# First tile of a fused attention and expert kernel: decoded weights grouped in pairs, and where their transfers are issued

## The chip, the cores and the metric

The kernel runs on one core of a Trainium2 chip. The metric is the device time of one execution in microseconds (us), as the median of several runs. The core has five engines that run their own instruction streams and wait for each other through semaphores: TensorE (PE, the matmuls), VectorE (DVE), ScalarE (ACT), GpSimd (POOL) and SyncE (SP, which here only starts DMAs). ACT can start DMAs too. Memory transfers are carried by 16 DMA engines that all queues share.

## The reference, cut to what matters

```
# attention without softmax: 8 batches, 8 heads, 576 tokens, head size 64
kv  = einsum('bhsd,bhse->bhde', k, v)
out = einsum('bhsd,bhde->bhse', q, kv)
x   = out / sqrt(mean(out*out) + 1e-6) * g_norm        # -> 4608 tokens x 512
# first expert layer: w_in 512 x 2048, w_out 2048 x 512
h = x @ w_in
P = a0 + a1*h + a2*h*h + a3*h*h*h
Q = 1 + |b0|*|h| + |b1|*h*h
x = (P / (Q + 1e-6)) @ w_out
# second expert layer: w_gate, w_val 512 x 1536, w_out 1536 x 512
g = x @ w_gate
return (g * sigmoid(g) * (x @ w_val)) @ w_out
```

All of it is float32.

## The kernel before, in words

**Tiles and steps.** The first expert layer goes over nine tiles of 512 tokens. One tile has 16 steps, one for each block of 128 hidden columns; a step s counts through all tiles. In step s, PE multiplies x with block f of w_in (`h_mm`), ACT and DVE compute P/Q from the sum in PSUM (`g_step`, `g_finish`), and two steps later (LAG = 2) PE multiplies the activated block `ghl` with block f of w_out (`y_mm`). Between them, `attn_*` prepares x of the next tile.

**Exact products.** A float32 operand is held as a high and a low part that PE takes in its fast float32 form; a product is three matmuls (high·high, low·high, high·low; lines 110 to 118). The low part is the operand less its high part: ACT copies the high part, and DVE or POOL subtracts.

**Weights.** They arrive as 64-bit numbers, 0.5 MB for a block of 512 values in each of 128 partitions, and are decoded on the chip in the first tile alone: an ACT pass (`w_exp`), a DVE shift (`w_shift`, TENSOR_SCALAR `wraw<-wraw`), a DVE join (`wa_joins`, SCALAR_TENSOR_TENSOR `wraw<-wraw`), then the high part on ACT (`wt<-wraw`) and the subtraction on DVE (`wt<-wraw,wt`), both in `w_hi`. Later tiles only read the decoded `wt`. `wa_sets` is the list of what is decoded together, one entry a step. Before, blocks i0 and i1 of w_in come in the head of the program, and entry s then holds block i(s+2) of w_in and block o(s) of w_out: one 1024 column shift, join and ACT pass, and for each block its own 512 column copy and subtraction.

**Blocks left whole.** The w_out blocks named in `WHOLE` (11, 12, 13) are not split in the first tile: one DVE join writes them as plain float32 (`wf`), their `ghl` is not split either, and the product is one matmul in float32 (line 501) in place of three fast ones. `w_halve` splits them in steps 4, 7 and 10 of the second tile, and `w_move` moves one by a DMA in step 12.

**Transfers.** `wa_fetch` starts the transfers of an entry. All are started from SP's queue, between the loads of `kvm`/`kvr` (k and v, for the kv products that run beside the first tile) and of `q` for the next tile. A tile name has buffers, and a load waits until its buffer was read for the last time.

**Order.** Nothing is scheduled by a tool: each engine runs its instructions in the order in which the code issues them (line 1143). In the loop over steps that is: `h_mm(s)`, `y_mm(s-2)`, the kv products, `g_step` (the activation of step s, with the joins, the `ghl` of step s-1, the copies and subtractions in between), and at the end of the step `wa_scale` (the ACT pass and the shift of the next entry) and `wa_fetch`.

Of the kernel before, what the change touches and what calls it, by code (L numbers as in the profile page):

```python
# [8 lines left out]
F32 = mybir.dt.float32  # L9
# [6 lines left out]
P = 128  # L16
# [25 lines left out]
def fused_kernel(ctx: ExitStack, tc: tile.TileContext, kv_main, kv_left, q_t, w_in, w_out, w_gate, w_val, w_o2, ab, g_norm, out):  # L42
# [38 lines left out]
    rows = w_p.tile([1, 3, P], F32, tag="w3", name="rows")  # L81
# [7 lines left out]
    for n in (18, 20, 22, 24, 26, 28, 3):  # L89
        w_p.tile([P, 2, N], F32, tag=f"w{n}", name="place")  # L90
    kvf = w_p.tile([P, HP, P], F32, tag="w31", name="kvf")

    def act(out, in_, func=AF.Copy, **kw):
        nc.scalar.activation(out=out, in_=in_, func=func, **kw)  # L94
# [25 lines left out]

    W = {}
    raws = []
    WHOLE = (11, 12, 13)

    def w_views(st):
        wi = st.bitcast(I32).rearrange("p (n two) -> p n two", two=2)
# [27 lines left out]
    ring_w = {}

    def w_tile(n):
        kind, f, _ = wa_src[n]
        if kind == "o" or f >= 2 * (RING - 4):
            return w_p.tile([P, 2, N], F32R, tag=f"w{n}", name="wt")
        if f % 2 == 0:  # L160
            ring_w[f // 2] = ring_p.tile([P, 2, 2, N], F32R, tag=f"r{f // 2}", name="wt")
        return ring_w[f // 2][:, f % 2]

    def w_hi(st, n, key, eng=nc.vector):
        wt = W[key] = w_tile(n)
        act(wt[:, 0, :], w_views(st)[2])
        return partial(sub, eng, wt[:, 1, :], w_views(st)[2], wt[:, 0, :])


    wa_src = [("i", f, w_in[f]) for f in range(LAG)]  # L170
    wa_sets = [(f,) for f in range(LAG)]
    for f in range(NF1):
        n = len(wa_src)
        wa_src += [("i", f + LAG, w_in[f + LAG])] if f + LAG < NF1 else []
        wa_src.append(("o", f, w_out[f]))
        wa_sets.append(tuple(range(n, len(wa_src))))
    wa_raw = ((at_p, "hl"), (s_p, "stg"), (at_p, "r0"), (w_p, "w5"), (w_p, "w7"), (x_p, "x11"))
    wa_home = [3, 4, *(5, 0, 1) * 4, 0, 1, 2, 1]
    wa_n = [0]

    def wa_fetch():
        if wa_n[0] < len(wa_sets):
            ns, (pool, tag) = wa_sets[wa_n[0]], wa_raw[wa_home[wa_n[0]]]
            r = pool.tile([P, 2 if tag in ("hl", "stg", "x11") else 1, N], I64, tag=tag, name="wraw")
            for j, n in enumerate(ns):
                nc.sync.dma_start(out=r[:, j, :], in_=wa_src[n][2])
            raws.append((ns, r[:, :len(ns), :].rearrange("p a n -> p (a n)")))
            wa_n[0] += 1

    def wa_hi(eng=nc.vector):  # L190

        ns, r = raws.pop(0)
        js = [(j, n) for j, n in enumerate(ns) if not whole(n)]
        return [partial(w_hi, r[:, j * N:j * N + N], n, wa_src[n][:2], eng) for j, n in js]

    def wa_scale(*parts):
        for _, r in raws[:1]:
            for part in parts or (w_exp, w_shift):
                part(r)

    def whole(n):
        kind, f, _ = wa_src[n]
        return kind == "o" and f in WHOLE

    def wa_joins():
        ops = []
        for ns, r in raws[:1]:
            if not any(whole(n) for n in ns):
                return join_ops([r])
            for j, n in enumerate(ns):  # L210
                lo, hi, _ = w_views(r[:, j * N:j * N + N])
                out = hi
                if whole(n):
                    wf = W[wa_src[n][:2]] = w_p.tile([P, N], F32, tag=f"w{n}", name="wf")
                    out = wf.bitcast(I32)
                ops.append(partial(stt, out, hi, 3, lo, ALU.logical_shift_left, ALU.bitwise_or))
        return ops

    def w_halve(f):
        wf, k = W["o", f], WHOLE.index(f)  # L220
        pool, tag = (w_p, f"w{2 * WHOLE[k - 1] + 3}") if k else (at_p, "r0")
        wt = W["o", f] = pool.tile([P, 2, N], F32R, tag=tag, name="wt")
        act(wt[:, 0, :], wf)
        return [partial(sub, nc.vector, wt[:, 1, :], wf, wt[:, 0, :])]

    def w_move():
        wf = W["o", WHOLE[0]]
        wt = W["o", WHOLE[0]] = w_p.tile([P, 2, N], F32R, tag=f"w{2 * WHOLE[-1] + 3}", name="wt")
        nc.sync.dma_start(out=wt.bitcast(F32), in_=wf.bitcast(F32))
# [19 lines left out]
    kv_lefts = [w_p.tile([P, HP, 2, P], F32, tag=f"w{n}", name="kvr") for n in (26, 27, 19)]

    def kv_tag(n):
        slots = (24, 25, 28, 29, 30, 20, 21, 22, 23)
        return f"w{slots[n] if n < 5 else slots[(n - 5) % 9] if n < 28 else (23, 24, 25, 28)[n - 28]}"

    def kv_load(k):

        for n in range(kv_n[0], min(kv_n[0] + k, len(kv_jobs))):
            b, hp = kv_jobs[n]
            tag = kv_tag(n)
            if kv_last.get(tag, -1) >= kv_n[1] or hp == 0 and kv_n[1] < 4 * b - 8:  # L260
                return
            kv_last[tag] = n
            m = w_p.tile([P, 4, 2, P], F32, tag=tag, name="kvm")
# [46 lines left out]
            nc.sync.dma_start(out=kvp[diag(j), 1 - j::2, :], in_=kvf[diag(1 - j), j::2, diag(1 - j)])  # L310

    def q_load(hp):
        q = q_in[0, hp] = w_p.tile([P, N], F32, tag=f"w{20 + hp}", name="q")
        nc.sync.dma_start(out=q, in_=q_t[0, hp])

    def q_load4(T, g):
# [136 lines left out]
    def attn_tail(c):  # L453
        T, f = at(c)
        if T is None:
            return
        if T == 1:
            if f == 2:
                kv_place()
            if f in (1, 4):  # L460
                q_load4(1, f // 3)
            elif f == 10:
                r_spread(1)
            elif f == 12:
# [62 lines left out]
    def g_finish(s, ops, his=()):  # L527
        if s not in mid:
            return []
        e1, e2, e3 = mid.pop(s)  # L530
        stt(e1, e1, 1.0 + EPS_Q, e2, ALU.add, ALU.mult)
        stt(e3, e3, na[:, 0:1], e2, ALU.add, ALU.mult)
        run(ops, len(ops))
        w = s in WHOLE
        hl = g_p.tile([P, N] if w else [P, 2, N], F32 if w else F32R, tag="g", name="ghl")
        stt(hl if w else e3, e1, 2.0, e3, ALU.subtract, ALU.mult)
        lows = [hi() for hi in his[:1]]
        if not w:
            split(hl, e3, nc.gpsimd)
        hl_t[s] = hl  # L540
        return lows + [hi() for hi in his[1:]]

    def g_step(s, joins=(), his=(), exps=(), acts=()):
        ps = ew.pop(s)
# [598 lines left out]
    with tc.manual_schedule():  # L1143
# [29 lines left out]

        pkv = ps_a.tile([P, HP, P], F32, tag="pa0", name="pkv")
        po, pss, nb = {}, {}, {}
        sq2 = w_p.tile([P, 2, N], F32, tag="w9", name="sq")
        w0, w1, w2 = raws[:3]
        w_x = {}

# [9 lines left out]
        def sq(i):  # L1189
            act(sq2[:, i % 2, :], po[i], AF.Square)  # L1190

        def ss(i):
            pool, tag = (ps_h, "ph") if i < HP - 1 else (ps_a, "pa1")
            pss[i] = ss_mm(sq2[:, i % 2, :], pool.tile([P, N], F32, tag=tag, name="ss"))
            ru = w_p.tile([P, 2, N], F32, tag=f"w{11 + 2 * i}", name="nb")
            nb[i] = (ru[:, 0, :], ru[:, 1, :])

        def norm_r(i):
# [41 lines left out]
        kv(2)  # L1240
        kv_load(2)
        wa_fetch()
        sq(1)
        norm_u(0)
        ss(1)
# [332 lines left out]
```

## Time and profile before

| what | us |
|---|---|
| median of 3 runs (lowest, highest) | 1649.77 (1649.67, 1651.23) |
| profiled execution, its own time | 1650.95 |
| its span, first to last instruction | 1649.2 |
| PE busy in the span | 1637.1 |
| DVE, ACT, POOL busy | 1366.8, 1028.6, 361.9 |

The profile is of one execution. A row of its time views has the start, the length, the engine, the line of the code and the operation with output, inputs and shape; in brackets stands how long the engine was idle before it, and what it waited for. A matmul's length includes its way through the array, and the next starts before it ends: 0.227 us after the one before, so lengths of matmuls are not added up. DVE and ACT overlap a little in the same way. Three engines are busy for most of the first tile (up to about 136 us); after that, PE is hardly ever idle until the last 50 us.

### The profile page before, as it was taken

What the parts mean: (1) busy time and instruction counts of PE and PEld (TensorE: products, weight loads), DVE (VectorE), ACT (ScalarE), POOL (GpSimd) and SP (SyncE); (2) the same over time, 40 slices, a digit from 0 to 9 for tenths busy, and PEclk for the clock granted to TensorE, in tenths of its full rate; (3) what the DMA queues carried; (4) which work ended last, traced back from release to release, by engine and by line L of the source; (5) the groups of instructions that cost most, each with busy time, mean ns of one, the idle gap of its engine ahead of it and who ended that gap; (6) DMA issues with size and microseconds to landing.
All of it is one profiled execution on the core that took longest, in us unless ns stands there. A gap on an engine that the chain in (4) does not pass through costs nothing.

```text
span 1649.2 us, 22608 instructions
## 1 busy us (share of the span) xinstructions
PE 1637.1 (99%) x8394; PEld 1348.8 (82%) x8394; DVE 1366.8 (83%) x1900; ACT 1028.6 (62%) x1713; POOL 361.9 (22%) x260
## 2 busy tenths in 40 slices
PE   8999999999999999999999999999999999999999
PEld 5776878878787878788888888888888888888888
DVE  7999888879798888989995766778568868999997
ACT  7988777777777776777774434445435456444443
POOL 2211322323232223323330102223202144000000
PEclk9999999999999999999999999999999999999999
DMA  9961112031212121111415237233494444444542
GB/s 352 371 225 64 40 59 70 26 90 39 65 51 90 52 77 52 57 47 64 163 68 192 77 110 285 76 136 109 151 331 145 152 160 160 143 136 150 154 138 87
DMA packets 82611, 206.67 MB, mean 125 GB/s; under 512 B 7555, under 2 KB 36484, under 8 KB 79812
## 3 DMA queue, kind: packets, MB, share of 16 engines
q1 hardware_dynamic: 82484, 205.21, 37.1%
q8 instruction: 66, 1.08, 0.3%
q14 instruction: 45, 0.37, 0.1%
q10 hardware_dynamic: 16, 0.02, 0.0%
HBM read 138.41 MB, written 66.19 MB: 124 GB/s over the span
## 4 chain that ended last, share of the span: by engine, by line
PE 92%; DMA 3%; DVE 3%; ACT 1%; issue 1%; SPq 0%; POOL 0%; DVEq 0%; ACTq 0%; POOLq 0%
PE y L495 19%; PE pb L1014 15%; PE pb L118 11%; PE pb L117 11%; PE pb L116 10%; PE ph L116 7%; PE ph L117 7%; PE ph L118 7%; DMA kvm<-in_kv_main 1%; PE y L112 1%; PE y L111 1%; PE y L110 1%; DMA wraw<-in_w_in 1%; PE po L332 1%; DVE e L107 1%; DMA wraw<-in_w_out 1%
## 5 line engine op out<-in xcount | busy, mean ns | idle before, releaser
L495 PE MATMUL y<-ghl,wt 128*128 128x512 f32 x1476 | 355.8, 390 | 0.0
L495 PEld LDWEIGHTS y<-ghl,wt 128*128 128x128 f32 x1476 | 276.3, 188 | 59.0 <-ACT wt L94 0.7
L118 PE MATMUL pb<-xc,wu 128*128 128x512 f32 (+1 forms) x804 | 303.8, 378 | 0.0
L116 PE MATMUL pb<-xc,wu 128*128 128x512 f32 (+1 forms) x804 | 303.8, 378 | 0.0
L117 PE MATMUL pb<-xc,wu 128*128 128x512 f32 (+1 forms) x804 | 303.7, 378 | 0.0
L97 POOL TENSOR_TENSOR ghl<-e,ghl 128x512 fp32r<-128x512 f32 x141 | 186.5, 1323 | 498.6 <-ACT ghl L94 343.6
L1014 PE MATMUL pb<-wo,xo 128*128 128x256 f32 (+1 forms) x1428 | 248.7, 336 | 0.0
L1014 PEld LDWEIGHTS pb<-wo,xo 128*128 128x128 f32 x1428 | 219.8, 190 | 28.7
L94 ACT ACTIVATE e<-pb 128x512 f32<-128x512 f32 (+1 forms) x162 | 92.7, 572 | 236.5 <-PE pb L118 236.2
L578 DVE TENSOR_TENSOR e<-e,pb 128x512 f32<-128x512 f32 (+1 forms) x216 | 140.5, 655 | 114.7 <-PE pb L118 64.4
L107 DVE SCALAR_TENSOR_TENSOR e<-e,e 128x512 f32<-128x512 f32 x285 | 211.7, 743 | 27.9 <-ACT e L94 22.6
L116 PE MATMUL ph<-x,wt 128*128 128x512 f32 x540 | 212.7, 394 | 0.0
L118 PE MATMUL ph<-x,wt 128*128 128x512 f32 x540 | 210.4, 390 | 0.2 <-DVE wt L97 0.2
L117 PE MATMUL ph<-x,wt 128*128 128x512 f32 x540 | 210.2, 389 | 0.0
L94 ACT ACTIVATE e<-ph 128x512 f32<-128x512 f32 x144 | 86.0, 597 | 156.0 <-PE ph L118 144.1
L116 PEld LDWEIGHTS pb<-xc,wu 128*128 128x128 f32 x804 | 151.1, 188 | 28.3
L117 PEld LDWEIGHTS pb<-xc,wu 128*128 128x128 f32 x804 | 151.1, 188 | 28.3
L118 PEld LDWEIGHTS pb<-xc,wu 128*128 128x128 f32 x804 | 151.0, 188 | 27.8
L107 DVE SCALAR_TENSOR_TENSOR e<-e,b_abs,e 128x512 f32<-128x512 f32 x144 | 113.8, 790 | 53.8 <-ACT e L94 53.0
L94 ACT ACTIVATE xo<-graw 128x768 fp32r<-128x768 f32 x122 | 99.4, 842 | 89.3 <-DVE graw L578 49.4
L116 PEld LDWEIGHTS ph<-x,wt 128*128 128x128 f32 x540 | 101.3, 188 | 31.0 <-DVE e L107 5.9
L97 DVE TENSOR_TENSOR xo<-graw,xo 128x768 fp32r<-128x768 f32 x120 | 114.1, 963 | 11.4 <-ACT xo L94 11.4
(137 smaller groups left out, 2469.8 us busy)
## 6 DMA issues: line engine op xcount, KB each, us to landing
graw<-gd SPq DMA_DIRECT2D x36, 768.0 KB
gd<-gout SPq DMA_DIRECT2D x96, 256.0 KB
kvm<-in_kv_main SPq DMA_DIRECT2D x32, 512.0 KB
yraw<-yd SPq DMA_DIRECT2D x22, 512.0 KB
q<-in_q_t SPq DMA_DIRECT2D x36, 256.0 KB
yd<-sb SPq DMA_DIRECT2D x18, 512.0 KB
out<-sb SPq DMA_DIRECT2D x17, 512.0 KB
wraw<-in_w_in SPq DMA_DIRECT2D x16, 512.0 KB
```

The source lines that it names most:

```text
L94: nc.scalar.activation(out=out, in_=in_, func=func, **kw)
L97: eng.tensor_tensor(out=out, in0=a, in1=b.bitcast(F32), op=ALU.subtract)
L107: nc.vector.scalar_tensor_tensor(out=out, in0=in0, scalar=scalar, in1=in1, op0=op0, op1=op1)
L110: nc.tensor.matmul(ps, lhsT=wh, rhs=xh, start=first, stop=False)
L111: nc.tensor.matmul(ps, lhsT=wl, rhs=xh, start=False, stop=False)
L112: nc.tensor.matmul(ps, lhsT=wh, rhs=xl, start=False, stop=last)
L116: nc.tensor.matmul(ps, lhsT=wh, rhs=xh, start=first, stop=False, skip_group_check=more)
L117: nc.tensor.matmul(ps, lhsT=wh, rhs=xl, start=False, stop=False, skip_group_check=more)
L118: nc.tensor.matmul(ps, lhsT=wl, rhs=xh, start=False, stop=last, skip_group_check=more)
L495: nc.tensor.matmul(yps[m], lhsT=w[:, a, c], rhs=g[:, b, :], start=False, stop=False)
L578: eng.tensor_tensor(out=out, in0=a, in1=b, op=op)
L1014: nc.tensor.matmul(out_, lhsT=x[:, hl, i, :], rhs=w, start=start and n == 0, stop=n == UP - 1, skip_group_check=True)
```

## The change

Five things are altered, nearly all in the first tile (steps 0 to 15) or ahead of it.

1. Entries of `wa_sets` hold two blocks of one matrix rather than one of each: i2 and i3, then o0 alone, o1 and o2, i4 and i5, o3 and o4, and so on to o13 and o14; o15 is last and alone. Copy and subtraction of an entry are one instruction over 1024 columns. An additional entry, o0, is decoded at the end of step 0 in one go. Step 14 has none.
2. `wa_fetch` is called with ACT's queue in the loop; an entry is one DMA of 1 MB rather than two of 0.5 MB. The four entries of the head stay on SP.
3. `WHOLE` is (13, 14): one 1024 column join for both, split by one `w_halve` in step 5 of the second tile. `w_move` is gone.
4. In the head, four matmuls whose result nothing reads follow the first quarter of `h_mm(0)`.
5. The copies and subtractions of a step (`his`) are issued after `ghl` is split, not the first of them before it. The q loads for the second tile's attention come in steps 2 and 5 rather than 1 and 4. The buffers in SBUF are grouped anew by `w_big`; kv loads take their buffers in pairs.

```diff
-    WHOLE = (11, 12, 13)
+    WHOLE = (13, 14)
...
+    def w_hi(st, key, eng=nc.vector):
+        t = w_pair(*key)
+        src = w_views(st)[2].rearrange("p (a n) -> p a n", a=2)
+        act(t[:, :, 0, :], src)
+        return partial(sub, eng, t[:, :, 1, :], src, t[:, :, 0, :])
...
-    wa_src = [("i", f, w_in[f]) for f in range(LAG)]
-    wa_sets = [(f,) for f in range(LAG)]
-    for f in range(NF1):
-        n = len(wa_src)
-        wa_src += [("i", f + LAG, w_in[f + LAG])] if f + LAG < NF1 else []
-        wa_src.append(("o", f, w_out[f]))
-        wa_sets.append(tuple(range(n, len(wa_src))))
-    wa_raw = ((at_p, "hl"), (s_p, "stg"), (at_p, "r0"), (w_p, "w5"), (w_p, "w7"), (x_p, "x11"))
+    wa_sets = [("i", 0), ("i", 1), ("i", 2), ("o", 0), ("o", 1)]
+    for f in range(4, NF1, 2):
+        wa_sets += [("i", f), ("o", f - 1)]
+    wa_sets += [None, ("o", NF1 - 1)]
+    ONES = (("i", 0), ("i", 1), ("o", 0), ("o", NF1 - 1))
+    wa_raw = ((at_p, "hl"), (s_p, "stg"), (x_p, "x11"), (at_p, "po"))
...
+        pool, tag = wa_raw[wa_home[n]]
+        r = pool.tile([P, 2, N], I64, tag=tag, name="wraw")
+        k = 1 if key in ONES else 2
+        src = (w_in if key[0] == "i" else w_out)[key[1]:key[1] + k]
+        eng.dma_start(out=r[:, :k, :], in_=src.rearrange("a p n -> p a n" if len(src.shape) == 3 else "a p k n -> p a (k n)"))
...
+        for key, r in raws[:1]:
+            if key and whole(key):
+                wf = at_p.tile([P, 2, N], F32, tag="r0", name="wf")
...
+                return [partial(stt, wf.bitcast(I32).rearrange("p a n -> p (a n)"), hi, 3, lo, ALU.logical_shift_left, ALU.bitwise_or)]
...
-            if f in (1, 4):
+            if f in (2, 5):
                 q_load4(1, f // 3)
...
-        lows = [hi() for hi in his[:1]]
         if not w:
             split(hl, e3, nc.gpsimd)
         hl_t[s] = hl
-        return lows + [hi() for hi in his[1:]]
+        return [hi() for hi in his]
...
         h_mm(0, (0,))
+        busy = ps_a.tile([P, N], F32, tag="pa0", name="busy")
+        for _ in range(4):
+            nc.tensor.matmul(busy, lhsT=W["i", 0][:, 0, :P], rhs=x_t[0, 0][:, 0, 0, :], start=True, stop=True)
...
-            elif t == 1 and f in halve_at:
-                acts.append(partial(w_halve, halve_at[f]) if f < 12 else w_move)
+            elif t == 1 and f == 5:
+                acts.append(w_halve)
...
             if t == 0:
-                if s:
-                    wa_scale()
-                wa_fetch()
+                wa_scale()
+                if not s:
+                    run(wa_joins())
+                    for hi in wa_hi():
+                        hi()()
+                wa_fetch(nc.scalar)
```

What stands on DVE around the end of step 0 (`e` are the activation's temporaries; the row with `b_abs` begins the activation of a step, the one with two inputs named `e` ends it). Before:

```order
32 L107 SCALAR_TENSOR_TENSOR e_405<-e_405,b_abs,e_406 128x512
33 L568 TENSOR_TENSOR e_407<-e_407,ph 128x512
34 L107 SCALAR_TENSOR_TENSOR e_407<-e_407,na,ph 128x512
35 L97 TENSOR_TENSOR wt<-wraw,wt 128x512 x2
36 L107 SCALAR_TENSOR_TENSOR e_405<-e_405,e_406 128x512
37 L107 SCALAR_TENSOR_TENSOR e_407<-e_407,na,e_406 128x512
38 L140 TENSOR_SCALAR wraw<-wraw 128x1024
39 L107 SCALAR_TENSOR_TENSOR wraw<-wraw 128x1024
40 L107 SCALAR_TENSOR_TENSOR e_407<-e_405,e_407 128x512
```

The same stretch after the change:

```order
32 L112 SCALAR_TENSOR_TENSOR e_400<-e_400,b_abs,e_401 128x512
33 L598 TENSOR_TENSOR e_402<-e_402,ph 128x512
34 L112 SCALAR_TENSOR_TENSOR e_402<-e_402,na,ph 128x512
35 L102 TENSOR_TENSOR wt<-wraw,wt 128x2x512
36 L145 TENSOR_SCALAR wraw<-wraw 128x512
37 L112 SCALAR_TENSOR_TENSOR wraw<-wraw 128x512
38 L102 TENSOR_TENSOR wt<-wraw,wt 128x512
39 L112 SCALAR_TENSOR_TENSOR e_400<-e_400,e_401 128x512
40 L112 SCALAR_TENSOR_TENSOR e_402<-e_402,na,e_401 128x512
41 L145 TENSOR_SCALAR wraw<-wraw 128x1024
42 L112 SCALAR_TENSOR_TENSOR wraw<-wraw 128x1024
43 L112 SCALAR_TENSOR_TENSOR e_402<-e_400,e_402 128x512
```

Three instructions of o0 stand ahead of the row that completes `e_402`, from which `ghl` of step 0 is made.

On ACT, from the activation of step 1 to that of step 2 (`kvc` empties the kv products, `ghl` is the high part of the activated block). Before:

```order
38 L94 ACTIVATE kvc<-pkv 64x256 x2
39 L94 ACTIVATE wt<-wraw 128x512
40 L94 ACTIVATE ghl<-e_407 128x512
41 L94 ACTIVATE wt<-wraw 128x512
42 L94 ACTIVATE e_465<-e_464,bias_q 128x512
43 L94 ACTIVATE e_465<-e_465 128x512
44 L94 ACTIVATE wraw<-wraw 128x1024
45 L94 ACTIVATE e_552<-ph 128x512
```

After:

```order
41 L99 ACTIVATE kvc<-pkv 64x256 x2
42 L99 ACTIVATE ghl<-e_402 128x512
43 L99 ACTIVATE wt<-wraw 128x2x512
44 L99 ACTIVATE e_461<-e_460,bias_q 128x512
45 L99 ACTIVATE e_461<-e_461 128x512
46 L99 ACTIVATE wraw<-wraw 128x1024
47 L216 DMA wraw<-in_w_out 128x2x512
48 L99 ACTIVATE e_541<-ph 128x512
```

`ghl` now precedes the copy of the weights, and the transfer of an entry is started behind the ACT pass of the entry before it.

On PE, the two products with whole blocks after the change (y_525 to y_537 are the four parts of the output tile; `po` belongs to the next tile's attention):

```order
393 L123 MATMUL ph<-x,wt 128x512
394 L532 MATMUL y_525<-ghl,wf 128x512
395 L532 MATMUL y_529<-ghl,wf 128x512
396 L532 MATMUL y_533<-ghl,wf 128x512
397 L532 MATMUL y_537<-ghl,wf 128x512
398 L363 MATMUL po<-q_1393,kvc 64x128 x4
399 L363 MATMUL po<-q_1393,kvc 64x384 x4
400 L115 MATMUL ph<-x,wt 128x512
```

The place is step 15, with block 13; block 14 follows in step 16, where before there were twelve matmuls of the fast form, and the `wf` rows of steps 13 and 14 are gone.

## Rows read from the trace of the kernel before

**Rows 1.** First part of the page: busy us (share of the span), instructions.
```profile
PE 1637.1 (99%) x8394; PEld 1348.8 (82%) x8394; DVE 1366.8 (83%) x1900; ACT 1028.6 (62%) x1713; POOL 361.9 (22%) x260
```

**Rows 2.** Busy time by stretch: length, engines' busy (instructions), clock, DMA share, GB/s.
```profile
25.00:131.00 106.00, 102.03 (x894) 77.83 (x892) 103.98 (x153) 92.95 (x155) 15.56 (x13) 1.00 0.84 293
140.00:1600.00 1460.00, 1460.00 (x6991) 1210.27 (x6990) 1202.11 (x1657) 894.17 (x1487) 337.43 (x233) 1.00 0.33 111
42.00:58.00 16.00, 15.20 (x169) 12.51 (x168) 14.51 (x21) 13.44 (x24) 3.97 (x4) 1.00 1.03 382
```

**Rows 3.** PE's time line: the head, step 2, and steps 13 to 16.
```profile
19.85 0.40 PE L112 MATMUL ph<-x,wt 128*128 128x512 f32 x1
21.51 0.50 PE L110 MATMUL ph<-x,wt 128*128 128x512 f32 x1 [1.26 <-ACT x L94]
...
35.77 0.50 PE L110 MATMUL y<-ghl,wt 128*128 128x512 f32 x1 [0.71 <-ACT ghl L94]
...
37.13 0.50 PE L112 MATMUL y<-ghl,wt 128*128 128x512 f32 x1 [0.63 <-POOL ghl L97]
...
116.50 3.59 PE L501 MATMUL y<-ghl,wf 128*128 128x512 f32 x8
...
122.43 0.39 PE L118 MATMUL ph<-x,wt 128*128 128x512 f32 x1
123.29 3.70 PE L501 MATMUL y<-ghl,wf 128*128 128x512 f32 x8 [0.47 <-DVE ghl L107]
...
131.26 3.70 PE L501 MATMUL y<-ghl,wf 128*128 128x512 f32 x8 [1.45 <-DVE ghl L107]
```

**Rows 4.** DVE's time line, 33 to 55 us and at step 14.
```profile
34.37 0.68 DVE L107 SCALAR_TENSOR_TENSOR e<-e,e 128x512 f32<-128x512 f32 x1
...
46.66 0.70 DVE L140 TENSOR_SCALAR wraw<-wraw 128x1024 int32<-128x1024 int32 x1 [1.42 <-DMA wraw<-in_w_out]
...
52.31 1.63 DVE L97 TENSOR_TENSOR wt<-wraw,wt 128x512 fp32r<-128x512 f32 x2
...
130.52 0.68 DVE L107 SCALAR_TENSOR_TENSOR ghl<-e,e 128x512 f32<-128x512 f32 x1
```

**Rows 5.** DVE by operation and shape, 24 to 131 us: busy us, mean ns.
```profile
L97 DVE TENSOR_TENSOR wt<-wraw,wt 128x512 fp32r<-128x512 f32 x26 | 19.3, 777 | 0.0
L107 DVE SCALAR_TENSOR_TENSOR wraw<-wraw 128x1024 int32<-128x1024 int32 x11 | 13.4, 1216 | 0.1
L140 DVE TENSOR_SCALAR wraw<-wraw 128x1024 int32<-128x1024 int32 x14 | 9.6, 686 | 1.4 <-DMA wraw<-in_w_out 1.4
L140 DVE TENSOR_SCALAR wraw<-wraw 128x512 int32<-128x512 int32 x1 | 0.4, 422 | 0.0
```

**Rows 6.** DVE by operation and shape, whole span: a subtraction over 1024 columns.
```profile
L97 DVE TENSOR_TENSOR xc<-yraw,xc 128x1024 fp32r<-128x1024 f32 x10 | 12.2, 1217 | 0.5
```

**Rows 7.** ACT's time line: a copy, DMAs started by ACT, a wait for weights.
```profile
34.48 0.69 ACT L94 ACTIVATE wt<-wraw 128x512 fp32r<-128x512 f32 x1 [0.52 <-DVE wraw L107]
...
97.31 1.18 ACT L94 ACTIVATE wraw<-wraw 128x1024 f32<-128x1024 f32 x1
97.58 1.36 ACTq L379 DMA_DIRECT2D rd<-sq  x4
98.99 0.60 ACT L94 ACTIVATE e<-ph 128x512 f32<-128x512 f32 x1 [0.49 <-DMA rd<-sq]
...
111.58 1.18 ACT L94 ACTIVATE wraw<-wraw 128x1024 f32<-128x1024 f32 x1 [0.22 <-DMA wraw<-in_w_out]
```

**Rows 8.** The chain of waits, 20 to 60 us: start, length, what.
```profile
35.42 11.15 DMA wraw<-in_w_out
```

**Rows 9.** SP's time line: the two transfers of one entry, started together.
```profile
105.63 0.33 SPq L186 DMA_DIRECT2D wraw<-in_w_in  x1
106.01 0.43 SPq L186 DMA_DIRECT2D wraw<-in_w_out  x1
```

**Rows 10.** POOL's time line: subtractions for the low part of ghl.
```profile
51.51 1.28 POOL L97 TENSOR_TENSOR ghl<-e,ghl 128x512 fp32r<-128x512 f32 x1 [6.12 <-PE pkv L284]
```

More of the change, by code (lines that the diff above doesn't have):

```diff
@@ L80, in fused_kernel, with w_big @@
     na = const.tile([P, 4], F32, name="na")
-    rows = w_p.tile([1, 3, P], F32, tag="w3", name="rows")
+    def w_big(tag, name, shape=(2, 2, N), dt=F32):
+        return w_p.tile([P, *shape], dt, tag=tag, name=name)
+    for tag in ("i5", "i6", "i7", *(f"o{k}" for k in range(1, 8)), "o0"):
+        w_big(tag, "place")
+    head_t = w_big("o1", "head")
+    rows = head_t[0:1, 1, 0, :3 * P].rearrange("o (k n) -> o k n", k=3)
     ab_raw = const.tile([P, 6], F32, name="ab_raw")
@@ L88, in fused_kernel @@
     kvc = at_p.tile([P, B - 1, HP, D], F32, name="kvc")
-    for n in (18, 20, 22, 24, 26, 28, 3):
-        w_p.tile([P, 2, N], F32, tag=f"w{n}", name="place")
-    kvf = w_p.tile([P, HP, P], F32, tag="w31", name="kvf")
+    left_t = [w_big(tag, "kvr", (2, HP, 2, P)) for tag in ("o7", "o6")]
+    kvf = left_t[1][:, 1, :2].rearrange("p a b n -> p (a b) n")
     def act(out, in_, func=AF.Copy, **kw):
@@ L152, in w_join, with w_pair @@
             op()
[L154 to L165, printed above, removed]
+    def w_pair(kind, f):
+        if kind == "i" and f < 2 * (RING - 4):
+            t = ring_p.tile([P, 2, 2, N], F32R, tag=f"r{f // 2}", name="wt")
+        else:
+            t = w_big(f"{kind}{(f + (kind == 'o')) // 2}", "wt", dt=F32R)
+        W[kind, f], W[kind, f + 1] = t[:, 0], t[:, 1]
+        return t
@@ L166, in w_hi, with w_hi_one @@
+    def w_hi_one(st, key, eng):
+        kind, f = key
+        if key == ("o", 0):
+            t = w_big("o0", "wt", dt=F32R)
+            W["o", 0], W["o", NF1 - 1] = t[:, 0], t[:, 1]
+        elif not f:
+            w_pair("i", 0)
+        wt = W[key]
         act(wt[:, 0, :], w_views(st)[2])
         return partial(sub, eng, wt[:, 1, :], w_views(st)[2], wt[:, 0, :])
-    wa_src = [("i", f, w_in[f]) for f in range(LAG)]
-    wa_sets = [(f,) for f in range(LAG)]
-    for f in range(NF1):
-        n = len(wa_src)
-        wa_src += [("i", f + LAG, w_in[f + LAG])] if f + LAG < NF1 else []
-        wa_src.append(("o", f, w_out[f]))
-        wa_sets.append(tuple(range(n, len(wa_src))))
@@ L177, in fused_kernel @@
-    wa_raw = ((at_p, "hl"), (s_p, "stg"), (at_p, "r0"), (w_p, "w5"), (w_p, "w7"), (x_p, "x11"))
-    wa_home = [3, 4, *(5, 0, 1) * 4, 0, 1, 2, 1]
-    wa_n = [0]
[L181 to L188, printed above, removed]
@@ L190, in wa_hi @@
-    def wa_hi(eng=nc.vector):
[L192 to L203, printed above, removed]
-    def wa_joins():
-        ops = []
-        for ns, r in raws[:1]:
-            if not any(whole(n) for n in ns):
-                return join_ops([r])
[L210 to L229, printed above, removed]
+    def w_hi(st, key, eng=nc.vector):
[3 more added lines that the diff above has]
+        return partial(sub, eng, t[:, :, 1, :], src, t[:, :, 0, :])
@@ new lines, in fused_kernel, with wa_fetch @@
+    wa_sets = [("i", 0), ("i", 1), ("i", 2), ("o", 0), ("o", 1)]
[4 more added lines that the diff above has]
+    wa_raw = ((at_p, "hl"), (s_p, "stg"), (x_p, "x11"), (at_p, "po"))
+    wa_home = [0, 0, 2, 3, *(0, 1, 2) * 3, 0, 1, 0, 1, 0, 0]
+    wa_n = [0]
+    def wa_fetch(eng=nc.sync):
+        n = wa_n[0]
+        if n == len(wa_sets):
+            return
+        wa_n[0] += 1
+        key = wa_sets[n]
+        if n < 2:
+            if not n:
+                raws.append(w_big("o0", "wraw", (2, N), I64))
+            r = raws[0][:, n]
+            nc.sync.dma_start(out=r, in_=w_in[n])
+            raws.append((key, r))
+            if n:
+                raws.pop(0)
+            return
+        if not key:
+            raws.append((None, None))
+            return
+        pool, tag = wa_raw[wa_home[n]]
[3 more added lines that the diff above has]
+        eng.dma_start(out=r[:, :k, :], in_=src.rearrange("a p n -> p a n" if len(src.shape) == 3 else "a p k n -> p a (k n)"))
+        raws.append((key, r[:, :k, :].rearrange("p a n -> p (a n)")))
@@ new lines, in wa_hi, with wa_scale, whole @@
+    def wa_hi(eng=nc.vector):
+        key, r = raws.pop(0)
+        if not key or whole(key):
+            return []
+        if key in ONES:
+            return [partial(w_hi_one, r, key, eng)]
+        return [partial(w_hi, r, key, eng)]
+    def wa_scale():
+        for key, r in raws[:1]:
+            if key:
+                w_exp(r)
+                w_shift(r)
+    def whole(key):
+        return key == ("o", WHOLE[0])
+    w_f = []
+    def wa_joins():
+        for key, r in raws[:1]:
+            if key and whole(key):
+                wf = at_p.tile([P, 2, N], F32, tag="r0", name="wf")
+                w_f.append(wf)
+                for j in range(2):
+                    W["o", WHOLE[j]] = wf[:, j, :]
+                lo, hi, _ = w_views(r)
+                return [partial(stt, wf.bitcast(I32).rearrange("p a n -> p (a n)"), hi, 3, lo, ALU.logical_shift_left, ALU.bitwise_or)]
+            if key:
+                return join_ops([r])
+        return []
@@ L232, in fused_kernel, with w_halve @@
+    def w_halve():
+        [wf] = w_f
+        t = w_pair("o", WHOLE[0])
+        act(t[:, :, 0, :], wf)
+        return [partial(sub, nc.vector, t[:, :, 1, :], wf, t[:, :, 0, :])]
     kv_in = {}
@@ L248, in fused_kernel @@
     kv_last = {}
[L249 to L253, printed above, removed]
+    kv_lefts = [left_t[0][:, 0], left_t[0][:, 1], left_t[1][:, 0]]
+    kv_tags = ("o4", "i5", "i6", "o5", "i7", "o3", "o4", "i5", "i6", "o5", "o5", "i6", "i7", "", "i7", "")
+    kv_t = {}
     def kv_load(k):
@@ L258, in kv_load @@
             b, hp = kv_jobs[n]
-            tag = kv_tag(n)
-            if kv_last.get(tag, -1) >= kv_n[1] or hp == 0 and kv_n[1] < 4 * b - 8:
+            tag = kv_tags[n // 2]
+            if n % 2 == 0 and kv_last.get(tag, -1) >= kv_n[1] or hp == 0 and kv_n[1] < 4 * b - 8:
                 return
             kv_last[tag] = n
-            m = w_p.tile([P, 4, 2, P], F32, tag=tag, name="kvm")
+            if not tag:
+                m = at_p.tile([P, 4, 2, P], F32, tag=("q", "r0")[n % 2], name="kvm")
+            else:
+                if n % 2 == 0:
+                    kv_t[0] = w_big(tag, "kvm", (2, 4, 2, P))
+                m = kv_t[0][:, n % 2]
             nc.sync.dma_start(out=m, in_=kv_main[b, hp])
@@ L312, in q_load @@
     def q_load(hp):
-        q = q_in[0, hp] = w_p.tile([P, N], F32, tag=f"w{20 + hp}", name="q")
+        if hp % 2 == 0:
+            q_in[0] = at_p.tile([P, 2, N], F32, tag=("q", "r0")[hp // 2], name="q")
+        q = q_in[0, hp] = q_in[0][:, hp % 2, :]
         nc.sync.dma_start(out=q, in_=q_t[0, hp])
@@ L1175, in fused_kernel @@
         po, pss, nb = {}, {}, {}
-        sq2 = w_p.tile([P, 2, N], F32, tag="w9", name="sq")
+        sq2 = head_t[:, 0]
         w0, w1, w2 = raws[:3]
@@ L1194, in ss @@
             pss[i] = ss_mm(sq2[:, i % 2, :], pool.tile([P, N], F32, tag=tag, name="ss"))
-            ru = w_p.tile([P, 2, N], F32, tag=f"w{11 + 2 * i}", name="nb")
+            if i % 2 == 0:
+                nb["t"] = w_big(f"o{2 + i // 2}", "nb")
+            ru = nb["t"][:, i % 2]
             nb[i] = (ru[:, 0, :], ru[:, 1, :])
@@ L1241, in fused_kernel @@
         kv_load(2)
+        wa_fetch()
         wa_fetch()
@@ L1302, in fused_kernel @@
         pkv = pkv1
-        halve_at = {4: 11, 7: 12, 10: 13, 12: None}
         kv_steps = {2: 2, 3: 2, 4: 4, 6: 4, 8: 4, 9: 4, 10: 2, 11: 2}
```

## The prediction

> **What bounds the kernel now.** First the page's busy times: PE works 1637.1 us of the span [rows 1], so at most some 12 us are to be had, wherever they lie. Then the busy times by stretch: from 140 to 1600 us PE is busy for 1460.00 of 1460 us; from 25 to 131 us it is busy for 102.03 of 106, and DVE for 103.98, with the clock at 1.00 [rows 2]. The reader is to see two engines that are both nearly full in the first tile, and one that is full after it. Then PE's time line, which says where PE's 4 us there are lost: 0.71 and 0.63 at the first block of `y`, then, after a long stretch without idle time, 0.47 and 1.45 in front of two whole blocks, both released by DVE's `ghl` [rows 3]. DVE's time line has `ghl` of step 13 at 130.52, and one wait of its own, 1.42 at 46.66 for a transfer [rows 4]. So DVE, with ACT beside it, sets when block 13 of `y` starts (131.26); from there on PE waits for nothing until the last 50 us. The time of the kernel is 131.26 plus PE's work behind it. What the change does to the time is: how much sooner or later DVE reaches `ghl` of step 13, plus what PE has to do more or less after that.
>
> **The change, part by part** (plus is later; distances between starts are used, a little shorter than the lengths).
>
> *The additional entry, o0, in step 0.* DVE gets a 512 column shift (0.42 long, 0.34 between starts), a join and a subtraction (0.68 long, 0.60 between starts each): 1.54 [rows 4, 5]. The pair's subtraction is one of 1.22, 1.14 between starts [rows 6], for two of 0.60, which gives back 0.06. Between join and subtraction DVE has nothing else: it waits for ACT's copy of 0.69 [rows 7], for which I take 0.65. Step 0 on DVE thus ends 1.54 - 0.06 + 0.65 = 2.13 later, and with it `ghl` of step 0 and the first `y`: PE's wait of 0.71 there becomes about 2.7. On DVE the wait of 1.42 at 46.66 lies behind this and absorbs as much, if the weights are there by then; two more pairs give back 0.16. Left: 2.13 - 1.42 - 0.16 = +0.55. From both sides: -0.8 if ACT's copy is hidden and the second handover too, +2.1 if the transfer is as late as before by the same amount.
>
> *Fewer instructions from there to `ghl` of step 13.* By the two orders there are 11 shifts of 1024 columns and one of 512 before, and 11 of 1024 after: -0.34. Joins: 8 of 1024 (1.14 between starts) and 7 of 512, 13.32, against 11 of 1024, 12.54: -0.78. Subtractions: 19 of 0.60 against 10 of 1.14, 11.40 each: 0. Sum -1.12 [rows 5, 6].
>
> *POOL's subtraction beside DVE's.* The 26 subtractions `wt` before last 777 ns in the mean [rows 5], where an undisturbed operation of 512 columns with operands in SBUF takes 0.68 [rows 4]: 26 x 0.097 = 2.5 us lost. The pair at 52.31 took 1.63, and POOL's own subtraction of 1.28 began at 51.51 and ended at 52.79 [rows 4, 10]: 0.48 of it lies beside the pair, and the pair is 0.3 longer than two undisturbed ones. After the change ACT makes `ghl` before the weights' copy, 0.6 earlier, so POOL falls under DVE's rows that read PSUM and is done when the subtraction comes. In the steps where ACT is late, a part stays. I take -1.0; the ends are -2.5 (all of it gone) and +0.5 (a subtraction over 1024 columns that is held up whole). The Trainium skill, SBUF — State Buffer, says of the port pair that the two engines share that it is an exclusive lock and that the loser fully blocks; the trace agrees (the pair is longer by about the overlap). By that rule alone the sum would be 1.5 lower than with my value.
>
> *Transfers from ACT.* Before, the entry that DVE waited for was started at 35.42 and needed 11.15 us [rows 8], but SP was far ahead. After, it is started behind the ACT pass of the entry before it, one step ahead of its use. A step is 6.8 (116.50 to 123.29) to 8.0 us (to 131.26) [rows 3]. An entry alone landed 111.58 - 105.63 = 5.95 after its start [rows 7, 9]. Beside a full queue of SP's loads at 382 GB/s [rows 2] half the rate is left to it: another 1 MB first, 2.6 us, makes 8.5 and 1.7 too late. SP's own loads in a step are some 1.25 MB (two kvm, half a kvr), 3.3 us, so mostly the queue runs dry in the middle; I count four entries in the saturated stretch at 0.4 each: +1.6. Ends: 0, and 4 x 1.7 = +6.8. The Trainium skill, DMA: Bandwidth & Descriptors, section "Issuing engines are not separate DMA queues", says that starting DMAs from several engines saves only the time to start them, since all end on the same 16 DMA engines and interleave; its section "Queues, rings and completion order" says that a DMA engine takes turns between queues, packet by packet. Before, ACT's queue carried nothing of size, so no run here shows the turns yet; by the first the transfers gain nothing, by the second half the rate as above.
>
> *Starting a DMA on ACT.* Four starts by ACT took 1.36 under an ACT pass of 1.18, and the next row of ACT was 0.49 late [rows 7]. One start a step is a quarter and is covered by the pass: 0. If it is not, 0.3 a step on ACT, which is idle for more than that: from 25 to 131 us 13 us in all [rows 2].
>
> *Whole blocks.* From 116.50 to the end of `h` at 122.43 + 0.23 are 6.16 us; twelve matmuls of `h` take 2.72, so a whole block takes 3.44, against 2.72 for a fast one: 0.72 more [rows 3]. Blocks 11 and 12 become fast, 1.44 less for PE, but ahead of the wait in front of block 13, so it is a longer wait and no gain. Block 14 becomes whole behind that wait: +0.72 (0.4 to 1.0).
>
> *No price.* The four unread matmuls: 0.91 in a gap from 20.08 to 21.51 [rows 3]. The one wide split in the second tile and the DMA that is gone there: PE waits for nothing there [rows 2], and DVE and ACT have idle time; 0, at the worst a few tenths once. The q loads go back one step on SP's queue, behind kv loads of the step before; they carry the same bytes and are read only by `po` in steps 5 and 7, two steps or more behind: 0; what they take from an entry in step 2 rather than 1 is in the bounds of the transfers.
>
> *Sum.* 0.55 - 1.12 - 1.0 + 1.6 + 0 + 0.72 = +0.75. Profiled execution: 1649.2 in the span and 1.75 around it, 1650.95; so 1651.7. It lies 1.2 above the median of the three runs, 1649.77, which I take as the base: 1650.5.
>
> **Rivals.**
>
> *The transfers are too late in every step (slower).* If an entry on ACT's queue takes as long as the one of 11.15 [rows 8], or waits behind SP's loads, each of the steps with saturated DMA waits 11.15 - 6.8 = 4.3 on ACT and then DVE; two to four such steps make +8 to +17, at most partly covered by PE's work in front: about 1660. It decides from 7 us on from start to landing. For it: one step of lead in place of two; against it: the lone entry at 5.95, and SP's queue has fewer transfers in it.
>
> *DVE's gains win (faster).* If the entries land in time (0 for 1.6), POOL's lock is gone (-2.5) and the copy of o0 is cheaper, DVE is some 4 us sooner, and PE becomes the bound. PE can gain no more than its idle time: 3.97 + 0.26 to 131.26, and 1.44 of the two fast blocks, less the 2.0 added in front of the first `y`, less 0.72 behind: -3.0. Half of it, 1648.3, is this rival's time.
>
> *PE's clock falls in the longer wait.* The 2.7 us before the first `y` are longer than any wait from 25 us on (1.45), after which the clock stayed at 1.00 [rows 2, 3]. At 1.2 GHz in place of 2.4, a few us of matmuls would take twice as long: +3, 1653.5. The fifth part, four matmuls in a gap of 1.4, lies 15 us ahead of it and does not help there.
>
> *Nothing changes in the end.* If DVE's gains are used up by o0 and the copy's waits exactly as far as the base has slack, +0.7 for block 14 or less: in the forecast's own range.
>
> **How the numbers follow.** My forecast with its bounds: 0.66, from -0.8 + 0 - 1.1 - 2.0 + 0.4, held at PE's bound, to 2.1 + 3 - 1.1 - 0.5 + 1: 1648 to 1654. Late transfers 0.14, of which a third stays under 1657. DVE's gains win 0.15, nearly all of it above 1647. The clock 0.05. The range 1647.4 to 1656.5 leaves out about 0.10 above and 0.05 to 0.1 below. A measurement tells 0.2%, 3.3 us, from no change: faster needs less than 1646.5, beyond PE's bound of -3.0: 0.06. Slower needs more than 1653.1: late transfers, half of the clock, an eighth of my own range: 0.22. The rest, 0.72, is the same.
>
> **What would show it.** In the profile after: `y` of step 0 starts near 37.8 with a wait of about 2.7 before it; DVE's wait of 1.42 near 46.7 is gone or smaller; waits of ACT for `wraw` stand at the ends of steps 1 to 4, some tenths each (right) or 2 to 4 us (the first rival); the subtractions over 1024 columns last 1.22 (lock gone) or up to 2 (not); the wait for `ghl` in front of the first whole block is 2 to 3 us and that block starts near 131.3; block 14 takes 3.4, and PE waits for nothing behind it. I am wrong if PE's waits in front of block 13 come from a transfer, or if block 13 starts more than 3 us from 131.3.

## The result, and the profile after

The changed kernel takes 1663.62 us in the median of four runs (1663.01 to 1666.58), beside 1649.72 for the kernel before. The ratio is 1.0081, with a 95% interval from 1.0069 to 1.0094: 13.9 us slower. The forecast was 1650.5 with a range to 1656.5, and the measured time lies outside it; the first of the rivals, the transfers that are too late in every step, is nearest to what came, with some of the third. The profiled execution took 1666.58 us, with a span of 1664.8. It is the slowest of the four, 3 us above the median, and differences between traces are read against its own span.

The chain of waits shows where the time goes. It is of the kernel after, from step 0 on (start, length, what; the rows left out are short ones between the transfers, three more transfers, and two stretches of ACT and DVE work, 67.66 to 74.94 and 92.72 to 98.85):

```profile
32.01 8.93 DMA wraw<-in_w_in
...
40.97 0.01 ACT wraw L99
40.97 9.27 DMA wraw<-in_w_out
...
50.27 9.41 DMA wraw<-in_w_in
...
59.72 7.94 DMA wraw<-in_w_out
...
108.81 8.74 DMA wraw<-in_w_out
...
117.63 10.15 DMA wraw<-in_w_in
```

A transfer lands, the ACT pass of its entry starts 0.03 us later, and in that moment the next transfer starts; that lasts 8 to 10 us, and so on. Nine transfers of weights stand in the chain between 32.01 and 127.78 us, with 82.1 us of 95.8: 9.1 each, where a step of the kernel before took 6.8 to 8.0. From 32.01 to 67.66, 35.7 us, the chain holds nothing else but these hand-overs. The two rows of ACT behind it (its time line; `ACTq` is a DMA that ACT starts):

```profile
40.97 1.21 ACT L99 ACTIVATE wraw<-wraw 128x1024 f32<-128x1024 f32 x1 [0.78 <-DMA wraw<-in_w_in]
40.97 0.42 ACTq L216 DMA_DIRECT2D wraw<-in_w_out  x1
```

The DMA stands behind the pass in ACT's order, and the pass waits for the entry before. So the next transfer can't start before the last one has landed: one is under way, never two. Two of the loop's transfers, started at 67.69 and 92.76, landed before ACT came to their pass, and the next ones, at 74.94 and 98.85, started when ACT got there. The loop starts twelve transfers of 1 MB and a last one of 0.5; five entries, one more than said above, come from SP in the head.

DVE's shifts of the weights from 24 to 131 us, beside the row of [rows 5] (busy, mean ns; idle before them, and for what):

```profile
L145 DVE TENSOR_SCALAR wraw<-wraw 128x1024 int32<-128x1024 int32 x13 | 9.0, 693 | 14.2 <-DMA wraw<-in_w_in 9.1 <-DMA wraw<-in_w_out 5.2
```

DVE waits 14.2 us for weights, in nine places, where it waited 1.4 in one: 12.8 more. (The expectations below have 15.5, which counts in a wait of 1.3 in the head of the program that the kernel before has too.) PE's time line, in the places of [rows 3]:

```profile
37.91 0.79 PE L115 MATMUL y<-ghl,wt 128*128 128x512 f32 x1 [3.16 <-ACT ghl L99]
...
132.21 4.59 PE L526 MATMUL y<-ghl,wt 128*128 128x512 f32 x12 [3.31 <-ACT ghl L99]
...
146.30 3.70 PE L532 MATMUL y<-ghl,wf 128*128 128x512 f32 x8 [0.22 <-DVE ghl L112]
...
153.84 3.60 PE L532 MATMUL y<-ghl,wf 128*128 128x512 f32 x8
```

Block 13 starts at 146.30 instead of 131.26, 15.0 later; the span is 15.6 longer. All of the difference but 0.6 is made ahead of block 13. The prediction's own sign of being wrong, a block 13 more than 3 us away from 131.3, is met.

Three stretches of the kernel after, by busy time (clock, DMA share and GB/s stand last):

```profile
39.00:42.00 3.00, 2.85 (x7) 2.16 (x7) 2.40 (x4) 2.18 (x3) 0.22 (x1) 0.50 0.13 30
...
72.00:75.00 3.00, 2.24 (x76) 2.24 (x78) 2.06 (x4) 2.97 (x6) 1.29 (x1) 1.00 0.00 0
...
113.00:116.00 3.00, 3.00 (x15) 2.47 (x14) 2.76 (x4) 2.94 (x5) 1.30 (x1) 1.00 0.13 47
```

Behind the wait of 3.16 the clock is at 0.50, the lower of its two levels; it fell again behind a wait of 2.41 for a load (0.58 from 108 to 111 us) and behind the wait of 3.31 (0.74 from 130 to 135). In the first and the last of these stretches a transfer of weights is under way (the rows of the chain at 32.01 and 108.81) while the DMA engines are 13% busy: its bulk has moved, its end has not come. In the second nothing moves: the transfer started at 67.69 has moved all of its 1 MB.

### The profile page after: what moved, and what is told of

It reads as the page before. It is cut to its first block, busy times and chain, and to the rows that moved or that the text cites. A ratio compares the mean times of both kernels' runs of the same rounds, so it can differ in the third digit from the quotient of the medians.

```text
span 1664.8 us, 22535 instructions
## 1 busy us (share of the span) xinstructions
PE 1643.8 (99%) x8402; PEld 1354.7 (81%) x8402; DVE 1362.9 (82%) x1883; ACT 1028.3 (62%) x1700; POOL 365.6 (22%) x261
## 4 chain that ended last, share of the span: by engine, by line
PE 91%; DMA 5%; DVE 2%; ACT 1%; issue 0%; SPq 0%; POOL 0%; DVEq 0%; POOLq 0%
PE y L526 18%; PE pb L1044 15%; PE pb L123 10%; PE pb L121 10%; PE pb L122 10%; PE ph L121 7%; PE ph L123 7%; PE ph L122 7%; DMA wraw<-in_w_in 3%; DMA wraw<-in_w_out 2%; PE y L115 1%; PE y L117 1%; PE y L116 1%; PE po L363 1%; PE ph L115 1%; DVE e L112 1%
## 5 line engine op out<-in xcount | busy, mean ns | idle before, releaser
L526 PE MATMUL y<-ghl,wt 128*128 128x512 f32 x1488 | 361.5, 392 | 4.1 <-ACT ghl L99 4.1
L526 PEld LDWEIGHTS y<-ghl,wt 128*128 128x128 f32 x1488 | 280.3, 189 | 65.1 <-ACT ghl L99 5.7
L608 DVE TENSOR_TENSOR e<-e,pb 128x512 f32<-128x512 f32 (+1 forms) x216 | 140.6, 655 | 115.5 <-PE pb L123 65.0
```

The source lines that it names most:

```text
L526: nc.tensor.matmul(yps[m], lhsT=w[:, a, c], rhs=g[:, b, :], start=False, stop=False)
L608: eng.tensor_tensor(out=out, in0=a, in1=b, op=op)
```

## The experiments

Three theories were set against each other: (1) pacing, as above; (2) ACT's queue is a slow one; (3) the pairs, o0 or the whole blocks cost it. Each ratio is to runs of the kernel before on the same chip, with its 95% interval.

**The loop's transfers on SP's queue again** (sp_queue).

```diff
-                wa_fetch(nc.scalar)
+                wa_fetch()
```

> The changed kernel with the loop's transfers started from SP's queue again, everything else as changed. Theory 1 (pacing): behind the ACT pass that waits for one entry, the next entry can't start, so a step of the first tile lasts as long as one landing, 7.8 to 10.2 us in the trace after; SP waits for no data, so the waits of 15.5 us on DVE go: 1649 to 1652 us. Theory 2 (ACT's queue gives slow transfers): also 1649 to 1652. Theory 3 (the pairs, o0 in step 0 or the whole blocks cost it): stays at 1661 to 1664.

Measured: 1654.74, ratio 1.0023 (1.0014 to 1.0033). Of the 0.81% this one word gives back 0.58%, some 9.6 us, though the time stays above the 1649 to 1652 that were expected; the waits of DVE for weights are down to one, of 2.68. Theory 3 has at most the 3.7 us that are left. Theory 2 is answered in the trace, by that one wait. SP's time line, then DVE's:

```profile
104.61 1.30 SPq L419 DMA_DIRECT2D r<-rd  x2
106.33 0.38 SPq L216 DMA_DIRECT2D wraw<-in_w_in  x1
```
```profile
115.80 0.69 DVE L145 TENSOR_SCALAR wraw<-wraw 128x1024 int32<-128x1024 int32 x1 [2.68 <-DMA wraw<-in_w_in]
```

Started by SP, a transfer of 1 MB also took 9.5 us. ACT's queue isn't the slower one; SP had started the others sooner, while this one stood behind `r<-rd` in SP's order.

**Ahead of the pass rather than behind it** (ahead).

```diff
             if t == 0:
+                if s:
+                    wa_fetch(nc.scalar)
                 wa_scale()
...
-                wa_fetch(nc.scalar)
+                    wa_fetch(nc.scalar)
```

> The changed kernel with each transfer still on ACT's queue, but issued just ahead of the ACT pass that waits for the entry before it, not just behind. Theory 1: a late entry no longer delays the start of the next one; with a landing of 9.2 us and a step of 6.9, waits of 2.3 come in every other step rather than in every one, so half of the 15.5 us go: 1655 to 1658 us. Theory 2: a landing is as slow as before and the start moves by little: 1661 to 1664. Theory 3: 1661 to 1664.

Measured: 1660.83, ratio 1.0067 (1.0052 to 1.0082). The waits of DVE for weights are 7.3 us in three places instead of 14.2 in nine, as pacing asks; the time comes back by 0.14% only, some 2.3 us, less than expected, and the interval overlaps that of the kernel after. The spans of the two profiled executions differ by 7.1 us (1664.8 and 1657.7), as the waits do, but one is the slowest run of its kernel and the other the fastest of its own. The direction fits, the size was missed. This edit breaks the link between a landing and the next start, and leaves one step of lead; so most of the 9.6 us isn't shown to hang on the link alone.

**Two entries under way, still on ACT's queue** (two_out).

```diff
-                wa_fetch(nc.scalar)
+                for _ in range(2 if not s else s != 9):
+                    wa_fetch(nc.scalar)
```

> The changed kernel with two entries under way on ACT's queue: two are started at the end of step 0, none at the end of step 9. Theory 1: an entry has two steps, 13.8 us, for a landing of 9.2: the waits for weights go, 1649 to 1652 us. Theory 2: if the queue gives 1 MB per 9 us whatever is outstanding, two entries land in 18 us, and a step still waits 2 us: 1660 to 1664. Theory 3: 1661 to 1664.

Measured: 1654.29, ratio 1.0023 (1.0013 to 1.0032), the same as with SP's queue. The queue, the size and the place of the transfers are those of the change; only the number under way, and with it the lead of two steps, differs. Theory 2 is out. Theory 1 is shown for 0.58% in this sense: one entry under way, one step ahead, is too little. The 1649 to 1652 that it expected did not come. DVE still waits 0.48 once early on, and 1.68 for the entry where the lead is one step again, started at 107.05:

```profile
115.50 0.69 DVE L145 TENSOR_SCALAR wraw<-wraw 128x1024 int32<-128x1024 int32 x1 [1.68 <-DMA wraw<-in_w_in]
```

**The kernel before with its transfers on ACT's queue** (before_act): `wa_fetch()` at the end of the loop becomes `wa_fetch(nc.scalar)`, two DMAs of 0.5 MB an entry.

> The kernel before with one edit: the loop's transfers are started from ACT's queue, behind the ACT pass, where the code had them on SP's. Theory 1: the same pacing comes into the kernel before: each step lasts one landing of 8 to 10 us, 1659 to 1666 us. Theory 2: the same. Theory 3: no difference, 1649 to 1651.

Measured: 1668.28, ratio 1.0108 (1.0093 to 1.0123). The one edit costs the kernel before at least as much as the whole change did, and 2 us more than the 1666 expected at most. DVE waits 15.1 us for weights, 5.96 in one place.

**Each entry as two DMAs of 0.5 MB** (after_split).

```diff
-        eng.dma_start(out=r[:, :k, :], in_=src.rearrange("a p n -> p a n" if len(src.shape) == 3 else "a p k n -> p a (k n)"))
+        for j in range(k):
+            eng.dma_start(out=r[:, j, :], in_=src[j] if len(src.shape) == 3 else src[j].rearrange("p k n -> p (k n)"))
```

> The changed kernel with each entry's 1 MB fetched by two DMAs of 0.5 MB, both on ACT's queue at the same place. If one wide DMA is what makes a landing take 9.2 us (two of 0.5 MB took 5.95 in the kernel before): the waits for weights shrink to less than a third, 1653 to 1656 us. Theory 1 alone (position on ACT's queue, one entry under way, whatever its form): 1661 to 1665.

Measured: 1665.84, ratio 1.0092 (1.0077 to 1.0108). Landings in its chain are 6.7 to 11.4 us. One DMA of 1 MB in place of two isn't the cause; the time is a little above the 1661 to 1665 of theory 1.

**What is left: 3.3 us above before.** Four edits of two_out, and one with two of them. First twelve unread matmuls ahead of the first `y` (two_fill), and the subtraction of o0 moved behind the row that completes `e` of step 0 (two_o0):

```diff
+                if s == LAG:
+                    busy = ps_a.tile([P, N], F32, tag="pa0", name="busy")
+                    for _ in range(12):
+                        nc.tensor.matmul(busy, lhsT=W["i", 0][:, 0, :P], rhs=x_t[0, 0][:, 0, 0, :], start=True, stop=True)
```
```diff
-                    for hi in wa_hi():
-                        hi()()
+                    o0_sub = [hi() for hi in wa_hi()]
...
+                if s == 1:
+                    his = [lambda: o0_sub[0], *his]
...
         lows = g_finish(s - 1, ops, his) + lows
+        if s == 1:
+            run(lows)
```

> The kernel with two entries under way on ACT's queue (3.3 us above the kernel before), and twelve more matmuls whose result nothing reads ahead of the first y, where PE waits 3.15 us. Clock theory: after that wait the matmuls of the first y stand 0.43 us apart for eight rows, not 0.23; filling the wait keeps the clock at 1.00 and gives back 1.6 us: 1.5 to 2 above before. Order theory (DVE is late anyway, the slow matmuls are covered): no change, 3.0 to 3.6 above.

> The same kernel with two entries under way, and the subtraction of o0 moved behind the row of DVE that completes step 0's e, so that DVE no longer waits for ACT's copy of o0 (0.73) nor subtracts (0.60) ahead of it. Clock and o0 theory: the first y starts 1.3 us sooner, PE's wait there is 1.8, the clock stays up: 1.3 to 2.9 us sooner, so 0.4 to 2.0 above before. Theory that the end is set by DVE at the whole blocks: no change, 3.0 to 3.6 above.

Measured: 1653.70, ratio 1.0018 (1.0009 to 1.0026), and 1654.14, ratio 1.0018 (1.0009 to 1.0027). Both are a little lower than two_out, neither clear of it, and above what the clock theory expected (1.5 to 2, and 0.4 to 2.0 us above before). Then both edits, with nine matmuls (two_both):

> Two entries under way, the subtraction of o0 moved as in two_o0, and nine unread matmuls ahead of the first y, whose wait was 2.5 us there. If the late first y and the clock behind it add up: 1.0 to 2.0 above before. If ACT and DVE set the steps behind it anyway (two_fill had a new wait of 1.43 for kvc there): as two_o0 and two_fill alone, 2.5 to 3.1 above before.

Measured: 1654.81, ratio 1.0022 (1.0013 to 1.0031). Nothing is gained. PE's clock and waits behind the first `y`, first two_out by stretch, then two_both by stretch, then two_both on PE's time line:

```profile
39.00:42.00 3.00, 2.47 (x7) 1.94 (x8) 2.52 (x4) 2.28 (x4) 0.47 (x1) 0.66 0.78 310
```
```profile
39.00:42.00 3.00, 2.53 (x11) 2.11 (x12) 2.25 (x3) 1.93 (x4) 0.42 (x1) 1.00 0.86 345
```
```profile
53.07 2.08 PE L313 MATMUL pkv<-kvm 128*64 128x64 f32 x64 [1.02 <-ACT kvc L99]
102.11 1.09 PE L313 MATMUL pkv<-kvm 128*64 128x64 f32 x29 [1.41 <-DMA kvm<-in_kv_main]
```

With the wait filled the clock stays at 1.00 (0.66 in two_out), so that mechanism is shown. But what PE gains it then spends waiting, 1.02 for ACT and 1.41 for a load, waits that are absent or shorter in two_out (none and 0.56 there). By these waits ACT and the loads set the pace there. The kernel before has such a wait too, 0.80 for ACT's `kvc` at 50.19, which the prediction's list of PE's waits leaves out.

Blocks 11 and 12 whole in place of 13 and 14 (two_whole), and no unread matmuls in the head (two_nobusy):

```diff
-    WHOLE = (13, 14)
+    WHOLE = (11, 12)
```

> The same kernel with two entries under way, and blocks 11 and 12 whole in place of 13 and 14. If PE is the bound up to step 13 and has 1.7 us of wait in front of block 11, the two whole blocks ahead lengthen nothing up to 1.44 and the two behind are 1.44 shorter: 1.4 us sooner, 1.9 above before. If DVE is the bound there: the split of 13 and 14 adds a subtraction and ACT's copy, 1.2 us on DVE: 0.2 us sooner.

> The same kernel with two entries under way, without the four unread matmuls of the head. If they only fill a gap: no change, 3.0 to 3.6 above before. If they keep the clock up in the head: up to 1 us later.

Measured: 1655.14, ratio 1.0026 (1.0016 to 1.0037), and 1654.81, ratio 1.0024 (1.0015 to 1.0033). Neither differs from two_out. The expected 1.4 us of the first did not come: PE waits 2.5 us for kv loads there, 1.4 in two_out; whether that is why isn't shown.

**The order of the copies alone, in the kernel before** (b_order), and with the later q loads (b_order_q):

```diff
-        lows = [hi() for hi in his[:1]]
         if not w:
             split(hl, e3, nc.gpsimd)
         hl_t[s] = hl
-        return lows + [hi() for hi in his[1:]]
+        return [hi() for hi in his]
```

> The kernel before with one part of the change: the copies and subtractions of the weights are issued after ghl is split, not the first ahead of it. POOL term of the prediction (DVE loses 2.5 us to POOL's subtraction beside its own, 1.0 to 2 of it given back, and DVE sets the start of the whole blocks): 0.7 to 1.5 us sooner than before, and the 26 subtractions last nearer 0.68 than 0.78. If the first block of h needs the weights that come later now: PE waits there, 0 to 1 us later.

> The kernel before with that order and the q loads in steps 2 and 5. If the wait of 1.42 us for weights at 46.66 comes from the q loads ahead of them on SP's queue, it goes, and another 0.5 us to 1 us with it: 1.0 to 2.5 sooner than before. If the q loads only shift the wait by a step: as with the order alone.

Measured: 1651.40, ratio 1.0004 (0.9996 to 1.0013), and 1651.13, ratio 1.0000 (0.9991 to 1.0009). The 26 subtractions in b_order, beside those of [rows 5]:

```profile
L97 DVE TENSOR_TENSOR wt<-wraw,wt 128x512 fp32r<-128x512 f32 x26 | 18.4, 741 | 0.4 <-ACT wt L94 0.4
```

They are 36 ns shorter, 0.9 us in all, but DVE waits 0.4 more for ACT's copies and 0.5 for another result of ACT (`sq`), and `ghl` of step 13 is at 130.51 where it was at 130.52. With the later q loads DVE's wait for weights is 0.9 in place of 1.4, and the time is the same. No version that was run is faster than the kernel before.

## Why the prediction was wrong, step by step

*Transfers from ACT: the step that failed.* The term was priced at +1.6, four entries that are 0.4 late each. The runs put it at 9.6 us (1.0081 against 1.0023). DVE's waits in the trace are nine, of 1.6 in the mean (14.2 us). So an entry was nearly as late as at the prediction's upper end, 1.7; what failed is the discount to 0.4, the count of four, and the assumption that late entries stop with the saturated stretch. Three things stand behind that.

The landing: the two figures that it was bounded with, 5.95 alone and 8.5 beside a full queue, were near. By the completion marks in the trace after, the three transfers of the loop with at most 0.1 MB of SP's loads beside them took 4.8 to 5.2 us (starts at 67.69, 92.76 and 127.86), and the nine in the chain, with 0.5 to 3.0 MB beside them, 9.1 in the mean. But the discount took it that SP's queue mostly runs dry; of twelve entries, nine met its loads. (Its 1.25 MB a step is 1.15 by the sizes on the page, which changes little.) The lead: one step, 6.8 to 8.0 us, is mostly shorter than such a landing, and the start stands behind a pass that waits for the entry before, so a late entry also makes the next one start late; the prediction had no term for that. The place: the chain's last landing starts at 117.63, long after the saturated stretch.

The Trainium skill, DMA: Bandwidth & Descriptors, section "Issuing engines are not separate DMA queues", says that transfers run on the same DMA engines whichever engine starts them; the runs agree, with 1.0023 from SP's queue and 1.0023 from ACT's with two under way. Half the rate beside SP's loads, as the prediction had it, is in the trace where both queues were full: from 87 to 91 us ACT's queue moved 0.85 MB and SP's 0.79.

The slower rival had the cause, transfers that are too late in every step, and a total, +8 to +17, that covers the 13.9. Its make-up was another: two to four waits of 4.3 in the steps with saturated DMA, where nine of 0.5 to 3.6 came on ACT, so the size is in part luck. Its chance of 0.14 was lower than the trace supported: the landing in the chain of waits, 11.15 [rows 8], was already over the 7 us at which it decides, and it was set aside because SP's queue was full in front of it. Two figures of the forecast's own also don't follow: PE's bound of -3.0 gives a lower end of 1646.8, not 1648, and the parts named for "slower" add up to 0.25, not 0.22. Neither touches the miss.

*The clock rival* came too: 3.16 us of wait, and 0.50 behind it. Its price was put at +3; in two_out, where the clock falls this once, filling the wait gave 0.7 us or nothing, as PE waits later instead. What the three falls cost in the kernel after isn't shown.

*The additional entry, o0*: the first `y` at 37.8 was forecast, after a wait of 2.7; it was at 37.91, after 3.16. DVE waited 0.72 for ACT's copy, forecast 0.65. What it costs at the end can't be told from the runs: two_o0 is lower than two_out by less than the interval.

*POOL's subtraction*: -1.0 was forecast, and b_order measured no change. The lengthening itself mostly goes: a subtraction over 1024 columns lasts 1.27 us in the mean after, near the 1.22 of [rows 6]. But with ACT's copy of both blocks behind `ghl`, DVE waits for ACT, 2.0 us from 24 to 131 us. In b_order the 0.9 us that the subtractions lose come back as 0.9 us of waits for ACT: the loss was exchanged, not removed.

*Whole blocks*: +0.72 was forecast. In two_out block 13 starts 2.74 later than before (134.00) and the next tile's second `po` 3.38 later (155.94 against 152.56): +0.64. In the kernel after, 15.6 of the span less 15.04: +0.56. The forecast was near.

*The unread matmuls, one DMA start a step on ACT, the wide split, the q loads*: nothing, as forecast; two_nobusy and b_order_q are even with what they were taken from, and no ACT row stands behind a DMA start of one entry.

Open: how the 3.3 us that two_out keeps are made up. Its trace has block 14 (0.6), 1.7 of a landing at 115.5, and a first `y` that is 2.4 later, but the edits that shorten the last did not give their time back. Open as well is why the transfer from 108.81 took 8.74 us with little beside it.

## What to carry to other kernels

A transfer that is issued from a compute engine's queue starts when that engine gets there: behind a pass that waits for the transfer before, the landing time, not the bandwidth, becomes the length of a step. Moving it ahead of that pass gave back 2.3 us here, a second transfer under way 9.6; so count first how many transfers can be under way, and compare the lead with a landing beside the other loads. SP's queue, which runs ahead, had two here, by nothing but its place. When a single measured landing is the floor of a sum, look for the slowest ones in the same trace and price them as the likeliest where another queue is in use.

## What the runs showed of the hardware

In the kernel after, 1 MB started by ACT landed 4.8 to 5.2 us after its start where SP's loads moved at most 0.1 MB meanwhile, and 7.8 to 10.2 us where they moved 0.5 to 3.0 MB; 1 MB at the 387 GB/s of one stretch is 2.7. One started by SP took 9.5 us. Traffic beside it isn't all: of the 8.74 from 108.81 the bulk moved at 387 GB/s from 111 to 113 us; in the 3 us from 113, the DMA engines were 13% busy, two of sixteen in the mean, and it landed at 117.55. The trace has sixteen completion marks for it: fourteen by 113.63, one at 114.47, the last at 117.55. So here the time of the transfer is that of its slowest share, and a mean rate says little on it. The transfer that landed at 40.94 had a shorter tail of this kind in the row from 39 to 42 us: fourteen marks by 39.38, then 40.32 and 40.94.
